# Two units' loads gated into each first projection, and the first two V casts written as a max over one element

## The chip, the cores and the metric

The kernel runs on one core of a Trainium2 chip. The metric is the device time of one execution in microseconds (us). Five engines run their own instruction streams: TensorE (PE, matmuls), VectorE (DVE), ScalarE (ACT), GpSimd (POOL) and SyncE (SP, which here only issues DMAs). They meet at semaphores. "PEld" is TensorE's weight load, which overlaps its matmuls.

## The reference

Cosine attention of 8 batches and 12 heads over 448 positions of 64, and then a feed-forward layer with the gate h·cos(h):

```python
q_n = q / (norm(q) + 1e-6);  k_n = k / (norm(k) + 1e-6)
attn = softmax(q_n @ k_n.T / 0.1)
x = (attn @ v)            # [8, 12, 448, 64] -> [3584, 768]
h = x @ w_in              # 768 -> 2048
out = (h * cos(h)) @ w_out   # 2048 -> 768
```

## The kernel before

**Units, pairs, batches.** The 12 heads of a batch are two *units* of six heads, 16 units in all (`u`); a unit is three *pairs* of heads, 48 pairs in all (`g`), six to a batch (`PB`). For a unit, `load(u, ...)` brings k and q into the f32 tile `raw[u % 2]` with two DMAs of 672 KB, and `load_v(u)` brings v into `vin[u % 2]` with one of 672 KB. All three are issued by SP. There are two buffers of each, so unit u + 2 can only be loaded when unit u's have been read.

**From raw to scores.** `norms` squares the pairs (`sq`, mostly on POOL, L686), sums the squares on DVE (`n`, L693), turns them into 1/norm with a Ln and an Exp on ACT (`lnn`, `rn`) and scales (`qks`, bf16, mostly on POOL, L712). From the tenth pair on (`BYPE`) a DMA transpose issued by SP makes `qkT` (L727); the first nine are transposed on PE and copied by DVE (L743). `scores` multiplies on PE (L752), ACT takes the exponent into `PX` (L757). `attend` multiplies with `va` (L774), which is v in bf16 with a column of ones; DVE divides by the sum (`rcp`, `xs`, L783 and L784), and a DMA transpose makes the pair's part of `xT` (L790), or PE and DVE do for every batch's last pair and the whole first batch (L798, L802).

**The V cast.** `copy_v(u)` converts `vin` to `va`. For the first two units that is a DVE `tensor_copy` (L662), for the others a POOL one.

**Projections.** `m1(b)`, the first projection, makes 96 matmuls for a batch (L815), in eight steps of twelve over three PSUM tiles (`SC0`, `SC1`, `AV`, the same tiles that scores and `attend` use); after each step ACT makes the cosine (`cosb`, L829) and DVE the product `gT` (L831). It runs at one place in the middle of the next batch's attention, after its second pair (`points`: pair 13 for batch 1, 19 for batch 2, and so on; batch 0's runs between the first batch and the second). `m2`, the second projection (L865), is put between the pieces of attention as filling work on PE, with its result copied by DVE to `osb` (L872) and stored by SP.

**What sets the order.** `Program` records every operation with its reads, writes and an assumed cost. `arrange` and `play` simulate the five engines and a shared DMA over these and fix, once, the order in which each engine runs its stream; among the operations that are ready, the one whose due time is earliest goes first. On the chip each engine then runs in that order, waiting at semaphores; nothing is reordered. Where the simulation sees PE idle for long, it puts matmuls of zeros there (`filler`, tile `zt`, L900), which compute nothing that is used: 92 of them. An edit of one operation therefore moves others all over the program.

**The loads' places.** The loads of the first two units come at the start. Those of units 2 and 3 follow the first batch, with the eight weight DMAs (POOL's queue, W1 and W2, f32 in memory and bf16 in SBUF). Unit 4 is loaded in pair 6. After that, units 5 to 15 are recorded one at a time, each in the second pair of the unit two before it, and go out as soon as their buffers are free.

Of the kernel before, what the change touches and what calls it, by code (L numbers as in the profile page):

```python
# [7 lines left out]
ALU = mybir.AluOpType  # L8
# [474 lines left out]
def bass_cosine_attention__then__act_gcu_kernel(  # L483
# [9 lines left out]
    B, NH, S, D = q.shape  # L493
# [121 lines left out]
    def dve(fn, reads, writes, cycles, lock=False, label="", bias=0.0):  # L615
        return P.op("DVE", fn, reads, writes, cost=0.15 + cycles / 960.0, lock=lock, label=label, bias=bias)
# [22 lines left out]
    def load(u, p0, p1, apart=False, eng="SP", behind=None):  # L639
        i = u % 2  # L640
        h = slice(2 * p0, 2 * p1)
        f = [lambda e, x=x, t=t: e.dma_start(
            rawv[i][:, h, NJ * x : NJ * x + NJ, :].rearrange("p h s d -> p h (s d)"), src(t, u, 2 * p0, 2 * (p1 - p0)))
            for x, t in enumerate((k, q))]
        for x in ((0,), (1,)) if apart else ((0, 1),):
            behind = P.ops[-1] if x == (1,) else behind
            behind = pooled[0] if eng == "POOL" else behind
            dma(eng, [f[y] for y in x], (), [("raw", i, p, y) for p in range(p0, p1) for y in x],
                "raw%d_%d_%s%s" % (i, p0, x, eng), 0.82 * (p1 - p0) * len(x), "load u%d p%d" % (u, p0), behind, 0.055)
            if eng == "POOL":  # L650
                pooled[0] = P.ops[-1]

    def load_v(u, eng="SP"):
        i = u % 2
        dma(eng, [lambda e: e.dma_start(vin[i].ap().rearrange("p (h c) -> p h c", h=UH), src(v, u, 0, UH))],
            (), [("vin", i)], "vin%d%s" % (i, eng), 2.4, "load v u%d" % u, pooled[0] if eng == "POOL" else None, 0.055)
        if eng == "POOL":
            pooled[0] = P.ops[-1]

    def copy_v(u):  # L660
        i = u % 2
        f = lambda e: e.tensor_copy(vav[i][:, :, 0:D], vinv[i])  # L662
        if u < 2:
            dve(f, [("vin", i)], [("va", i)], UH * NJ * D, label="va%d" % u)
        else:
            pool(f, [("vin", i)], [("va", i)], 1.46, label="va%d" % u)

# [136 lines left out]
    def m1(b, early=0, split=NKC, turn=TURN):  # L804
        table(SINSET)

        def names(gi):
            return [PHs[turn[gi]][0]]

        def step(gi, a, c0, c1):  # L810
            n, ph = 2 * gi + a, PHs[turn[gi]][1]

            def f(e):
                for c in range(c0, c1):
                    t = e.matmul(ph[:, a, 0:S], W1v[:, c, 128 * n : 128 * n + 128], xTv[b % 2][:, c, :],  # L815
                                 start=(c == 0), stop=(c == NKC - 1))
                return t

            P.op("PE", f, [("W1", n // 4)] + [("xT", b % 2, c) for c in range(c0, c1)], names(gi), cost=(c1 - c0) * MM,
                 mode="F", label="M1 %d.%d" % (b, n))  # L820

        for gi in range(early):
            for a in range(2):
                step(gi, a, 0, split)
        for gi in range(NF // 2):
            ph, cz = PHs[turn[gi]][1], gi % 2
            for a in range(2):
                step(gi, a, split if gi < early else 0, NKC)
            act(lambda e, ph=ph, cz=cz: e.activation(cosv[cz], ph[:, :, 0:S], ACT.Sin, bias=cst.ap()[:, 0:1], scale=1.0),  # L829
                names(gi) + ["cst0"], [("cos", cz)], 2 * S, "S", 1, label="sin%d.%d" % (b, gi))  # L830
            dve(lambda e, ph=ph, cz=cz, gi=gi: e.tensor_tensor(  # L831
                gTv[:, 2 * gi : 2 * gi + 2, S * (b % 2) : S * (b % 2) + S], ph[:, :, 0:S], cosv[cz], ALU.mult),
                names(gi) + [("cos", cz)], [("gT", b % 2, gi)], 2 * S, label="g%d.%d" % (b, gi))
        table(EXPSET)
# [48 lines left out]
    def after(o, *ops):  # L883
        for y in ops:
            o.deps.append((y, True))
# [49 lines left out]
    def pair(g):  # L935
        u, p = g // UP, g % UP
        if p == 0 and u >= 2 and u + 1 < NU:
            norms(u + 1, 0)
        grouped(both, g, 0)
        if g >= 1 and g != PB:  # L940
            attend(g - 1)
        if p == 0 and 2 <= u < NU - 1:
            copy_v(u + 1)
            if u == 2:
                load(4, 0, UP)
                load_v(4)
        if 3 <= u < NU - 2 and p == 1:
            load(u + 2, 0, UP)
            load_v(u + 2)
        if g + 2 < PB:  # L950
            norms((g + 2) // UP, (g + 2) % UP)
        if g + 1 < PB:
            grouped(transposes, g + 1)
        if BYPE <= g + 3 < NG:
            transposes(g + 3)
        grouped(both, g, 2)
# [34 lines left out]
    for g in range(PB, NG):  # L991
        pair(g)
        if g in points:
            m1(points[g])
            m2_add(points[g])
            m2_emit(None if points[g] < B - 2 else 8)
    attend(NG - 1)
# [42 lines left out]
```

## Time and profile before

| what | us |
|---|---|
| runs shown | 461.44, 462.76, 466.6 (median 462.76) |
| the profiled execution's own time | 465.73 |
| its span (first to last instruction) | 463.9 |
| PE busy, share of the span | 435.5, 94% |
| ACT, DVE, POOL busy | 263.5, 216.5, 195.0 |
| matmuls of zeros | 92, 23.6 us of PE's busy time |

The columns of the views that the prediction quotes are these. A *group* has line, engine, operation, output <- input, shapes, count, then busy us and mean ns of one, and the idle time of the engine just before them with what ended it. A *timeline* row has start (us from the span's start), length, engine, line, operation, tiles, count, and in brackets the idle time before it with what ended that. A *wait* row says who waited for whom: us in all, times, longest. A *window* row has the stretch A:B, its length, busy us (count) of the engines asked for, the clock that TensorE was granted (1.00 is full), the busy share of the DMA engines and GB/s. SPq is SP's stream of DMA issues; the time of such a row is that of issuing, not of the transfer. Buffer numbers are left out, so that `raw<-in_q_dram` is q of any unit.

The program falls into stages by what PE does: 0 to 45 us the first batch's attention, 45 to 66 the first projection of batch 0, then by turns the attention of a batch (about 28 us) and a first projection (about 20 us), which start at 104.2, 154.6, 207.4, 254.8, 303.4 and 352.7 us; from 396 us on the last projections.

### The profile page before, as it was taken

What the parts mean: (1) busy time and instruction counts of PE and PEld (TensorE: products, weight loads), DVE (VectorE), ACT (ScalarE), POOL (GpSimd) and SP (SyncE); (2) the same over time, 40 slices, a digit from 0 to 9 for tenths busy, and PEclk for the clock granted to TensorE, in tenths of its full rate; (3) what the DMA queues carried; (4) which work ended last, traced back from release to release, by engine and by line L of the source; (5) the groups of instructions that cost most, each with busy time, mean ns of one, the idle gap of its engine ahead of it and who ended that gap; (6) DMA issues with size and microseconds to landing.
All of it is one profiled execution on the core that took longest, in us unless ns stands there. A gap on an engine that the chain in (4) does not pass through costs nothing.

```text
span 463.9 us, 8849 instructions
## 1 busy us (share of the span) xinstructions
PE 435.5 (94%) x3800; PEld 235.8 (51%) x3800; DVE 216.5 (47%) x295; ACT 263.5 (57%) x319; POOL 195.0 (42%) x120
## 2 busy tenths in 40 slices
PE   8688999998899889999998999989999999999996
PEld 4355545554455435555554445545555555555663
DVE  4685672654732663356434562356431442244121
ACT  4467469874488537754678358743886168423000
POOL 1967448784475444673096309442560000000000
PEclk9799999999999999999999999989999999999999
DMA  8999994999349923992169806990481103101232
GB/s 221 236 236 220 248 253 96 279 187 245 98 65 256 210 65 72 232 239 90 37 144 227 223 0 132 224 236 4 86 137 52 36 8 92 45 0 35 79 92 69
DMA packets 95911, 63.87 MB, mean 138 GB/s; under 512 B 54912, under 2 KB 92288, under 8 KB 95872
## 3 DMA queue, kind: packets, MB, share of 16 engines
q1 hardware_dynamic: 90624, 57.02, 53.6%
q0 software_dynamic: 5248, 6.29, 7.8%
q8 instruction: 30, 0.49, 0.5%
q14 instruction: 9, 0.07, 0.1%
HBM read 45.61 MB, written 11.01 MB: 122 GB/s over the span
## 4 chain that ended last, share of the span: by engine, by line
PE 57%; DMA 14%; ACT 10%; DVE 7%; POOL 5%; issue 3%; SPq 3%; ACTq 0%
PE PO L865 20%; DMA raw<-in_q_dram 11%; PE SC L815 10%; PE AV L815 8%; PE AV L774 8%; PE SC L752 6%; ACT PX L757 6%; POOL qks L712 3%; DMA xT<-xs 3%; PE PO L900 2%; PE SC L865 2%; DVE gT L831 2%; DVE va L662 2%; SPq L727 2%; DVE n L693 2%
## 5 line engine op out<-in xcount | busy, mean ns | idle before, releaser
L757 ACT ACTIVATE PX<-SC 112x896 bf16<-112x896 f32 x192 | 164.8, 913 | 39.2 <-PE SC L752 39.0
L865 PE MATMUL PO<-W,gT 128*128 128x384 bf16 x816 | 148.8, 326 | 0.0
L712 POOL TENSOR_TENSOR qks<-raw,rn 112x1024 bf16<-112x1024 f32 x47 | 89.0, 1918 | 92.6 <-ACT rn L704 92.6
L815 PE MATMUL SC<-xT,W 128*128 128x448 bf16 x480 | 97.2, 357 | 8.8 <-DMA xT<-xs 6.9
L865 PEld LDWEIGHTS PO<-W,gT 128*128 128x128 bf16 x816 | 73.4, 98 | 57.4 <-issue 15.3
L686 POOL TENSOR_TENSOR sq<-raw 112x1024 bf16<-112x1024 f32 x42 | 78.5, 1892 | 41.1 <-DMA raw<-in_q_dram 41.1
L829 ACT ACTIVATE cosb<-SC,cst 128x896 f32<-128x896 f32 x40 | 40.2, 1006 | 68.1 <-PE SC L815 53.0
L815 PEld LDWEIGHTS SC<-xT,W 128*128 128x128 bf16 x480 | 46.4, 99 | 55.1 <-issue 14.4
L693 DVE TENSOR_REDUCE n<-sq 112x16 f32<-112x1024 bf16 (+1 forms) x49 | 58.3, 1192 | 33.6 <-POOL sq L686 27.2
L752 PE MATMUL SC<-qkT 64*128 64x448 bf16 x384 | 58.2, 358 | 7.1 <-DVE qkT L743 4.6
L815 PE MATMUL AV<-xT,W 128*128 128x448 bf16 x288 | 58.5, 352 | 5.2 <-DVE gT L831 4.8
L774 PE MATMUL AV<-va,PX 112*128 112x65 bf16 x1536 | 58.0, 194 | 1.6 <-DVE xT L802 1.2
L774 PEld LDWEIGHTS AV<-va,PX 112*128 112x128 bf16 x1536 | 52.5, 98 | 12.6 <-issue 10.8
L872 DVE COPY osb<-PO 128x384 f32<-128x384 f32 x51 | 28.2, 553 | 60.6 <-PE PO L865 60.5
L831 DVE TENSOR_TENSOR gT<-SC,cosb 128x896 bf16<-128x896 f32 x40 | 43.4, 1087 | 27.8 <-ACT cosb L829 24.1
L783 DVE RECIPROCAL rcp<-AV 112x8 f32<-112x8 f32 x48 | 9.9, 207 | 87.5 <-PE AV L774 87.5
L829 ACT ACTIVATE cosb<-AV,cst 128x896 f32<-128x896 f32 x24 | 24.2, 1007 | 40.0 <-PE AV L815 29.3
L815 PEld LDWEIGHTS AV<-xT,W 128*128 128x128 bf16 x288 | 27.4, 98 | 33.6 <-issue 7.1
L752 PEld LDWEIGHTS SC<-qkT 64*128 64x128 bf16 x384 | 15.0, 93 | 43.2 <-ACT PX L757 22.2
L784 DVE TENSOR_TENSOR xs<-AV,rcp 112x512 bf16<-112x512 f32 x48 | 33.2, 691 | 2.0
L831 DVE TENSOR_TENSOR gT<-AV,cosb 128x896 bf16<-128x896 f32 x24 | 26.1, 1086 | 17.1 <-ACT cosb L829 13.0
L662 POOL CAST va<-vin 112x1536 bf16<-112x1536 f32 x14 | 20.5, 1462 | 18.5 <-PE AV L774 17.9
(34 smaller groups left out, 143.4 us busy)
## 6 DMA issues: line engine op xcount, KB each, us to landing
vin<-in_v_dram SPq DMA_DIRECT2D x16, 672.0 KB, 8.2
raw<-in_k_dram SPq DMA_DIRECT2D x14, 672.0 KB, 5.9
raw<-in_q_dram SPq DMA_DIRECT2D x14, 672.0 KB, 8.4
W<-in_moe_w_in_dram POOLq DMA_DIRECT2D x4, 768.0 KB, 18.5
W<-in_moe_w_out_dram POOLq DMA_DIRECT2D x4, 768.0 KB, 18.9
out_dram<-osb SPq DMA_DIRECT2D x8, 336.0 KB, 3.1
out_dram<-osb SPq DMA_DIRECT2D x8, 288.0 KB, 2.7
out_dram<-osb SPq DMA_DIRECT2D x8, 240.0 KB, 3.0
```

Of the source, the lines that this page charges most:

```text
L662: f = lambda e: e.tensor_copy(vav[i][:, :, 0:D], vinv[i])
L686: pool(lambda e, x=x, y=y: e.tensor_tensor(y, x, x, ALU.mult), src_, dst, 0.1 + n * 1.78e-3, label="sq%d.%d" % (u, p))
L693: dve(lambda e, w=w: e.tensor_reduce(out=n2v[i][:, 2 * p : 2 * p + 2, w], in_=sqv[p][:, :, w, :], axis=mybir.AxisListType.X, op=ALU.add), ...
L712: f = lambda e, s0=s0, s1=s1: e.tensor_tensor(qksv[i][:, p, s0:s1, :, :].rearrange("p s h d -> p h s d"), rawv[i][:, h, s0:s1, :], bass.AP ...
L752: t = e.matmul(SCv[z][:, a, 0:S], qkT[k].ap()[r, NP * c : NP * c + 128], qkT[k].ap()[r, S : 2 * S], start=True, stop=True)
L757: act(lambda e: e.activation(PXv[j][:, c, 0 : 2 * S].rearrange("p (a s) -> p a s", a=2), SCv[z][0:NP, :, 0:S], ACT.Exp, scale=1.0 / TAU), ...
L774: t = e.matmul(AVv[:, a, n * x : n * x + n], PXv[j][:, c, k : k + 128], vav[i][:, NJ * (2 * p + a) + c, 0:n], start=(c == 0), stop=(c == N ...
L784: dve(lambda e: e.tensor_tensor(xsv[y].rearrange("p x h d -> p h x d"), AXv[:, :, :, 0:D], bass.AP(rcp[y], 0, [[NS, NP], [NJ, 2], [1, NJ], ...
L815: t = e.matmul(ph[:, a, 0:S], W1v[:, c, 128 * n : 128 * n + 128], xTv[b % 2][:, c, :], start=(c == 0), stop=(c == NKC - 1))
L829: act(lambda e, ph=ph, cz=cz: e.activation(cosv[cz], ph[:, :, 0:S], ACT.Sin, bias=cst.ap()[:, 0:1], scale=1.0), names(gi) + ["cst0"], [("c ...
L831: dve(lambda e, ph=ph, cz=cz, gi=gi: e.tensor_tensor(gTv[:, 2 * gi : 2 * gi + 2, S * (b % 2) : S * (b % 2) + S], ph[:, :, 0:S], cosv[cz], ...
L865: r = e.matmul(po[:, 0:HW], gTv[:, y, col : col + 128], W2v[:, y, HW * hf : HW * hf + HW], start=(y == 0), stop=(y == NF - 1))
```

## The change

Two edits.

1. The loads of units 6 to 15 are no longer issued one unit at a time as their buffers come free. They are recorded two units at a time behind `m1(points[g])`, units 6 and 7 in the first projection of batch 1, 8 and 9 in that of batch 2, up to 14 and 15 in that of batch 5, and each waits for the first step of that projection on PE (`after`). Units 0 to 5 stay as they were.
2. The first two V casts, DVE `tensor_copy` with f32 in and bf16 out, become `tensor_reduce` with max over an axis of one element: same input, same output, same values.

```diff
         if u < 2:
-            dve(f, [("vin", i)], [("va", i)], UH * NJ * D, label="va%d" % u)
+            dve(lambda e: e.tensor_reduce(
+                out=vav[i][:, :, 0:D], in_=vin[i].ap().rearrange("p (x d o) -> p x d o", d=D, o=1),
+                axis=mybir.AxisListType.X, op=ALU.max), [("vin", i)], [("va", i)], UH * NJ * D, label="va%d" % u)
         else:
...
-        if 3 <= u < NU - 2 and p == 1:
-            load(u + 2, 0, UP)
-            load_v(u + 2)
+        if u == 3 and p == 1:
+            load(5, 0, UP)
+            load_v(5)
...
         if g in points:
+            first = len(P.ops)
             m1(points[g])
+            first = [o for o in P.ops[first:] if o.eng == "PE"][0]
+            for u in (2 * points[g] + 4, 2 * points[g] + 5):
+                if u < NU:
+                    load(u, 0, UP)
+                    after(P.ops[-1], first)
+                    load_v(u)
+                    after(P.ops[-1], first)
             m2_add(points[g])
```

The assumed cost of the V cast is the same in both (`dve` with the same number of cycles). How the rows stand now, at three places; line numbers in the changed program are two higher from L664 on.

DVE in the first batch, around the first V cast (`qkT1` is the second pair's transposed q and k, `xs0` the first pair's result). Before:

```order
L743 COPY qkT0<-PO2 128x896
L662 CAST va0<-vin0 112x24x64
L743 COPY qkT1<-PO2 128x896
L783 RECIPROCAL rcp0<-AV 112x8
L693 TENSOR_REDUCE n21<-sq0 112x16
```

and with the change:

```order
L745 COPY qkT0<-PO2 128x896
L664 TENSOR_REDUCE va0<-vin0 112x24x64
L745 COPY qkT1<-PO2 128x896
L785 RECIPROCAL rcp0<-AV 112x8
L695 TENSOR_REDUCE n21<-sq0 112x16
```

Nothing moves here; the cast has another form. The second cast moves by one place: it stood ahead of the third copy to `xT0` and now stands behind it.

SP around the first projection of batch 2 (`xT0<-xs3` and `xT0<-xs4` are the parts of `xT` that this projection needs last, `raw0` and `raw1` units 8 and 9). Before:

```order
L790 DMA_TRANSPOSE xT0<-xs3 128x4x112
L642 DMA raw0<-in_k_dram 112x6x256
L642 DMA raw0<-in_q_dram 112x6x256
L727 DMA_TRANSPOSE qkT3<-qks1 128x8x112
L727 DMA_TRANSPOSE qkT4<-qks1 128x8x112
L790 DMA_TRANSPOSE xT0<-xs4 128x4x112
L727 DMA_TRANSPOSE qkT5<-qks1 128x8x112
L642 DMA raw1<-in_k_dram 112x6x256
L642 DMA raw1<-in_q_dram 112x6x256
L655 DMA vin1<-in_v_dram 112x6x256
```

and with the change, where the loads wait for the projection's first step:

```order
L792 DMA_TRANSPOSE xT0<-xs3 128x4x112
L729 DMA_TRANSPOSE qkT3<-qks1 128x8x112
L792 DMA_TRANSPOSE xT0<-xs4 128x4x112
L729 DMA_TRANSPOSE qkT4<-qks1 128x8x112
L729 DMA_TRANSPOSE qkT5<-qks1 128x8x112
L878 DMA out_0_dram<-osb0 48x768
L878 DMA out_0_dram<-osb0 80x768
L792 DMA_TRANSPOSE xT1<-xs0 128x4x112
L642 DMA raw0<-in_k_dram 112x6x256
L642 DMA raw0<-in_q_dram 112x6x256
L655 DMA vin0<-in_v_dram 112x6x256
L642 DMA raw1<-in_k_dram 112x6x256
```

Unit 8's load stood three transposes ahead of `xT0<-xs4` and unit 9's close behind it; both now stand behind all transposes of this attention.

DVE in the same projection (`n20` and `n21` are the sums of squares of the even and the odd unit, the eight `gT` the steps of the projection). Before:

```order
L693 TENSOR_REDUCE n20<-sq1 112x16
L693 TENSOR_REDUCE n20<-sq2 112x16
L831 TENSOR_TENSOR gT<-SC0,cosb0 128x2x448
L831 TENSOR_TENSOR gT<-SC1,cosb1 128x2x448
L693 TENSOR_REDUCE n21<-sq0 112x16
L831 TENSOR_TENSOR gT<-AV,cosb0 128x2x448
L693 TENSOR_REDUCE n21<-sq1 112x16
L831 TENSOR_TENSOR gT<-SC0,cosb1 128x2x448
L693 TENSOR_REDUCE n21<-sq2 112x16
L831 TENSOR_TENSOR gT<-SC1,cosb0 128x2x448
```

and with the change:

```order
L833 TENSOR_TENSOR gT<-SC0,cosb0 128x2x448
L833 TENSOR_TENSOR gT<-SC1,cosb1 128x2x448
L833 TENSOR_TENSOR gT<-AV,cosb0 128x2x448
L833 TENSOR_TENSOR gT<-SC0,cosb1 128x2x448
L833 TENSOR_TENSOR gT<-SC1,cosb0 128x2x448
L695 TENSOR_REDUCE n20<-sq0 112x16
L833 TENSOR_TENSOR gT<-AV,cosb1 128x2x448
L695 TENSOR_REDUCE n20<-sq1 112x16
L833 TENSOR_TENSOR gT<-SC0,cosb0 128x2x448
L695 TENSOR_REDUCE n20<-sq2 112x16
```

The even unit's sums move from ahead of the projection to behind its fifth step, and the odd unit's three move out of the projection, to the first three pairs after it. On POOL the odd unit's third squaring now stands behind two scalings of the even unit and a V cast; on ACT the odd unit's Ln (`lnn1`) now stands in the third pair after the projection, between its second and third exponent, where it stood in the first. PE's program has 78 matmuls of zeros instead of 92: 11 instead of 20 behind the first projection of batch 0, three fewer ahead of the very first transpose.

## The prediction, on record before the run

> **What bounds the kernel now.** I read the page first, then who waited for whom, then busy time by stages, then the timelines of the stages in which PE stands still.
>
> The page's row on PE:
>
> ```profile
> PE 435.5 (94%) x3800; PEld 235.8 (51%) x3800; DVE 216.5 (47%) x295; ACT 263.5 (57%) x319; POOL 195.0 (42%) x120
> ```
>
> PE bounds the kernel: of 463.9 us it is idle for 28.4. So the question is where it is idle, or busy with zeros, and whether the change fills that. From the list of waits, four rows (us in total, times, longest):
>
> ```profile
> PE SC L815 <- DMA xT<-xs: 6.9, 4, 2.2
> ...
> PE AV L815 <- DVE gT L831: 4.8, 5, 1.6
> PE SC L752 <- DVE qkT L743: 4.6, 3, 4.0
> ...
> PE SC L815 <- DVE gT L831: 1.5, 1, 1.5
> ```
>
> Three kinds of wait hold most of the idle time. A first projection waits for its input `xT` (6.9), its steps wait for DVE's `gT` to give back a PSUM tile (4.8 + 1.5), and at the start the scores wait for a DVE copy (4.6). Each has a place.
>
> The start, timelines of DVE, POOL, ACT and PE in that order:
>
> ```profile
> 13.25 6.46 DVE L662 CAST va<-vin 112x1536 bf16<-112x1536 f32 x1
> 19.64 0.61 DVE L743 COPY qkT<-PO 128x896 bf16<-128x896 bf16 x1
> ...
> 28.97 2.66 DVE L662 CAST va<-vin 112x1536 bf16<-112x1536 f32 x1
> ...
> 32.38 1.20 DVE L693 TENSOR_REDUCE n<-sq 112x16 f32<-112x1024 bf16 x1
> ```
>
> ```profile
> 16.66 1.90 POOL L686 TENSOR_TENSOR sq<-raw 112x1024 bf16<-112x1024 f32 x1
> 18.50 2.45 POOL L889 DMA_DIRECT2D W<-in_moe_w_in_dram  x2
> ...
> 30.77 2.62 POOL L712 TENSOR_TENSOR qks<-raw,rn 112x1024 bf16<-112x1024 f32 x1
> ```
>
> ```profile
> 13.96 3.34 ACT L757 ACTIVATE PX<-SC 112x896 bf16<-112x896 f32 x4 [1.25 <-PE SC L752]
> ...
> 20.99 1.90 ACT L757 ACTIVATE PX<-SC 112x896 bf16<-112x896 f32 x2 [3.69 <-PE SC L752]
> ```
>
> ```profile
> 21.86 1.94 PE L774 MATMUL AV<-va,PX 112*128 112x65 bf16 x32
> ...
> 26.89 1.19 PE L774 MATMUL AV<-va,PX 112*128 112x65 bf16 x32
> ```
>
> The first V cast takes 6.46 us and ends at 19.71, 1.15 us after POOL's squaring ends at 18.56: it stood waiting for POOL. The copy that the second pair's scores need is behind it, and ACT has no exponent to do for 3.69 us. A sum (TENSOR_REDUCE), on the other hand, ran at 32.38 for 1.20 us in the middle of a POOL instruction (30.77 to 33.39), not longer than its mean below: that form does not wait.
>
> The projections, from PE's timeline: those of batches 2 and 5, and that of batch 6, ahead of which no load is left.
>
> ```profile
> 154.58 4.70 PE L815 MATMUL SC<-xT,W 128*128 128x448 bf16 x24 [1.77 <-DMA xT<-xs]
> ...
> 303.39 6.38 PE L815 MATMUL SC<-xT,W 128*128 128x448 bf16 x24 [2.20 <-DMA xT<-xs]
> ...
> 352.67 4.70 PE L815 MATMUL SC<-xT,W 128*128 128x448 bf16 x24 [0.16 <-ACT PX L757]
> ```
>
> All four `xT` waits stand ahead of batches with a load of 2 MB in flight in the pairs before; without loads 0.16 us is left. And inside batch 2's projection, from the chain of waits and from DVE's timeline:
>
> ```profile
> 154.11 9.25 DMA raw<-in_q_dram
> ```
>
> ```profile
> 165.35 1.22 DVE L693 TENSOR_REDUCE n<-sq 112x16 f32<-112x1024 bf16 x1 [3.90 <-POOL sq L686]
> 166.49 1.08 DVE L831 TENSOR_TENSOR gT<-AV,cosb 128x896 bf16<-128x896 f32 x1
> ```
>
> Unit 9's q lands 9.25 us after its issue, POOL squares, and DVE, which runs in order, stands at the sum for 3.90 us with a finished projection step behind it. That is the gT wait.
>
> **Part 1, the V casts.** The price of the new form, from the groups by shape:
>
> ```profile
> L693 DVE TENSOR_REDUCE n<-sq 112x16 f32<-112x1024 bf16 x47 | 56.9, 1213 | 30.7 <-POOL sq L686 27.2 <-ACT sq L682 3.4
> ...
> L693 DVE TENSOR_REDUCE n<-sq 112x8 f32<-112x512 bf16 x2 | 1.4, 686 | 2.9 <-ACT sq L682 2.8
> ```
>
> 512 elements more cost 527 ns, 1.03 ns each; 1536 elements give 1213 + 527 = 1.74 us. These rows make one output of 64 inputs; the new form makes 1536 outputs of one. If an output cost as much as an input it would be 1.74 + 1.58 = 3.3 us; below 1.74 nothing speaks for it. I take 1.74, since eight outputs more are not seen in the step between the two rows. The cast then runs from 13.25 to 15.0, and the copy of the second pair's `qkT` ends at 15.6. What is late next is ACT: its four exponents of the first pair end at 17.30, so the next begin there instead of at 20.99, 3.7 us earlier. Behind the stall PE ran at half clock:
>
> ```profile
> 22.00:24.00 2.00, 2.00 (x37) 0.50 1.17 247
> 305.00:307.00 2.00, 2.00 (x7) 0.50 1.10 313
> ```
>
> (window rows; the clock is the figure after the count). The first AV block took 1.94 us instead of the 1.19 of the next: 0.75 more. I take 3.7 + 0.75 = **4.5 us**. Bounds: 5.9, if all of the second cast (2.66 - 1.74 = 0.9) and the three matmuls of zeros that go from the very start (0.5) count too; 0, if the front is held by its transfers (first rival).
>
> The Trainium skill, "VectorE: DVE Perf Modes", section "The perf-mode tier table", speaks against this edit: a tensor_reduce has no fast mode, where an f32 copy in SBUF runs two elements a cycle. By that alone each cast would lose some 0.8 us, an estimate from that page's factor of two on 1.74, and the sum would be 1.6 worse; in this trace the first cast took 6.46, so the slower form is the shorter one. Its page "SBUF — State Buffer", section "Who interferes with whom", gives a reason that agrees with the 6.46 and the 1.20: such a copy and GpSimd lock each other out of a shared port for a whole instruction, and a tensor_reduce on trn2 never takes it.
>
> **Part 2, matmuls of zeros.** The same rows by stage, of L900 alone:
>
> ```profile
> 66.30:104.20 37.90, 4.38 (x20) 1.71 (x20) 1.00 0.82 192
> ```
>
> 20 of them, 4.38 us, stand behind batch 0's projection, in a stage in which PE has work of the second projection to do; with the change 11 are left, 9 x 0.219 = **2.0 us** less. Bounds 0 (PE then waits at that place, for weights) and 2.0.
>
> **Part 3, the moved loads.** What goes: the four `xT` waits, 6.9 less 4 x 0.16 = **6.3**, since behind the change each attention looks as that before 352.67; bounds 3.5 (half) and 6.9. The gT waits, 6.3 less the one of batch 0's projection, which keeps its loads:
>
> ```profile
> 63.96 2.43 PE L815 MATMUL AV<-xT,W 128*128 128x448 bf16 x12 [0.74 <-DVE gT L831]
> ```
>
> so 6.3 - 0.7 = **5.6**, bounds 2.8 (half) and 5.6: no sum stands ahead of the fifth `gT` any more. And at 303.39 the 24 matmuls took 6.38 instead of 4.70, at the half clock of the second window row above, behind the longest of the `xT` waits: **1.7**, bounds 0 and 1.7. "TensorE: Matmul & The Clock Gate", section "What's actually happening" of the Trainium skill, ties half clock to an idle window of about 3.4 us; by that the 2.20 us wait was no cause, the 1.7 would stay, and the gain would be 16.9 instead of 18.6. Here the clock fell behind 2.20 and not behind 1.77, so I keep it.
>
> What comes: loads wait on PE at SP. Queued behind them on SP are only stores and the transposes of pairs after the projection, so nobody waits for that. The new place is late for the units, though. When does the odd unit land? The rate in batch 1's projection:
>
> ```profile
> 112.00:120.00 8.00, 7.27 (x39) 1.00 1.09 278
> ```
>
> The gate opens after twelve matmuls, 12 x 0.19 (24 in the 4.70 above) = 2.3 us into the projection. The size of one transfer, from the page's DMA issues:
>
> ```profile
> raw<-in_k_dram SPq DMA_DIRECT2D x14, 672.0 KB, 5.9
> ```
>
> Up to the odd unit's q there are five, 3.44 MB, at 278 GB/s 12.4 us, and some 2 us of latency (my allowance): 16.7. POOL squares twice, 3.8: 20.5 us after the projection's start. Then POOL's new order:
>
> ```profile
> 130.58 3.76 POOL L712 TENSOR_TENSOR qks<-raw,rn 112x1024 bf16<-112x1024 f32 x2 [8.04 <-ACT rn L704]
> 134.28 1.46 POOL L662 CAST va<-vin 112x1536 bf16<-112x1536 f32 x1
> ```
>
> and PE's third pair behind that projection, which ended at 125.7:
>
> ```profile
> 136.27 0.66 PE L752 MATMUL SC<-qkT 64*128 64x448 bf16 x4
> ```
>
> The scalings start 4.9 us after the projection's end, at 23.1 with its 18.2 us (96 x 0.19), so the squares are there 2.6 us early. Two scalings, the V cast, the third square (1.90) and the sum (1.21) end 13.2 after the projection's end; ACT's Ln for it stands behind two exponents of the third pair, whose scores start 10.6 after; with 0.4 for the first two of these matmuls and 1.90 for two exponents (the row at 20.99) ACT comes there at 12.9. It waits 0.3 us, five times: **1.5** lost; bounds 0, if PE has filling work meanwhile, and 5 x 1 = 5.
>
> Sum: 4.5 + 2.0 + 6.3 + 5.6 + 1.7 - 1.5 = **18.6 us**. The profiled execution took 465.73 us, so its like would take 447.1, with a span of 445.3. It lies 3.0 above the median of the runs shown, 462.76, by which I predict: 462.76 - 18.6 = 444.2.
>
> **Rivals.**
>
> *The front is held by transfers.* For: by the page's 40 slices of 11.6 us (busy tenths) the DMA engines have next to no pause in the first six, and unit 3's load, which batch 0's projection sums, is slow; the second row is from the chain of waits:
>
> ```profile
> DMA  8999994999349923992169806990481103101232
> ```
>
> ```profile
> 39.16 19.20 DMA raw<-in_q_dram
> ```
>
> Against: it is issued when POOL has scaled the first batch, which moves forward with the rest. If it lands at 58.4 all the same, DVE's sums hold batch 0's projection and the 4.5 are gone: gain 14.1, 448.7.
>
> *The `xT` waits stay*, because other transposes and not the loads hold SP's queue: gain 18.6 - 6.3 - 1.7 = 10.6, 452.2. Against it stands 352.67.
>
> *The odd unit is late, slower than before.* Loads pile up in one place; beyond 2.6 us of lateness each us moves ACT's Ln and the exponents behind it in five batches. Decisive point: to lose the 18.6 and 4.6 more (1%) takes 23.2 / 5 = 4.6 on top, 7.2 in all, so 3.44 MB in 19.6 us, 175 GB/s instead of 278. Then 467.4 or more. No saturated stretch quoted here is that slow; batch 1's attention shows 192 with a DMA share of 0.82.
>
> *It does not do what it says.* The order is a plan; if PE's other neighbours (ACT, POOL) close the gaps that open, the gain is the front's at most and lost again: 462.
>
> **How the numbers follow.** Forecast 0.57, front held 0.15, `xT` waits stay 0.12, no change 0.09, odd unit late 0.07. A difference of 1% is about what these runs can tell from none. Faster by over 1%, below 458.1: the first three, 0.84. Same 0.09, slower 0.07. All upper ends give 5.9 + 2.0 + 6.9 + 5.6 + 1.7 = 22.1, 440.7, and 1.3 less for the spread of the runs below their median: 439. The upper end must hold the second and third cases with half a gT wait lost (452.2 + 2.8): 455. Outside lie the last two cases.
>
> **What would show it.** The first cast: one row near 1.7 us, and ACT's second exponents near 17.3. The wait row of PE for `xT`: under 1 us. That for gT: about 0.7. Stages of first projections near 18.4 us. PE's granted clock 1.00 in all of them. A wait of ACT's `lnn` for DVE's `n` in the third pair behind each projection, near 0.3 us. It is wrong if the wait for raw's transfers moves onto ACT, or if PE waits for scores behind the projections.

## The result and the profile after

On the same chip the kernel before took 463.83 us (median; 461.44 to 466.6) and the changed kernel 446.51 us (445.1 to 447.41). The ratio is 0.962, 95% interval 0.956 to 0.969: 17.3 us less. The prediction was 444.2, with 439 to 455 as its range. The profiled execution took 445.67 us, 20.06 less than that of before (465.73), and its span is 443.9 instead of 463.9. The steps are compared on these two spans, 20.0 us apart.

The page's row on PE, of after:

```profile
PE 428.4 (97%) x3786; PEld 232.1 (52%) x3786; DVE 211.0 (48%) x295; ACT 264.2 (60%) x319; POOL 193.7 (44%) x120
```

PE is idle for 15.5 us instead of 28.4, and busy for 7.1 less. The list of waits of after:

```profile
PE SC L754 <- ACT PX L759: 3.5, 7, 1.8
...
PE SC L817 <- ACT PX L759: 1.1, 7, 0.2
...
PE SC L817 <- DVE gT L833: 0.4, 1, 0.4
```

The `xT` waits (6.9) are gone. Of the gT waits (4.8 + 1.5) there is 0.4 left, in batch 0's projection, whose loads were not moved. One row is larger than before: PE waits for ACT's exponents, once for 1.8 us.

The front, DVE's timeline and then PE's, of after:

```profile
12.18 1.74 DVE L664 TENSOR_REDUCE va<-vin 112x1536 bf16<-112x1536 f32 x1
13.84 0.62 DVE L745 COPY qkT<-PO 128x896 bf16<-128x896 bf16 x1
...
24.14 1.74 DVE L664 TENSOR_REDUCE va<-vin 112x1536 bf16<-112x1536 f32 x1
```

```profile
58.31 2.43 PE L817 MATMUL AV<-xT,W 128*128 128x448 bf16 x12
...
145.16 4.70 PE L817 MATMUL SC<-xT,W 128*128 128x448 bf16 x24 [0.16 <-ACT PX L759]
...
283.50 4.70 PE L817 MATMUL SC<-xT,W 128*128 128x448 bf16 x24 [0.16 <-ACT PX L759]
```

Each cast is one row of 1.74 us. The last twelve matmuls of batch 0's projection stand at 58.31; before they stood at 63.96. The later projections, here those of batches 2 and 5, begin behind a wait of 0.16 us.

The windows of PE by stage (the columns after the stretch are its length, PE's busy time with its count, granted clock, DMA share, GB/s): batch 1's attention, then everything from its projection to the start of batch 6's, then the rest. Before:

```profile
66.39:104.24 37.85, 37.03 (x408) 1.00 0.82 193
104.24:352.67 248.43, 234.89 (x2138) 0.99 0.66 143
352.67:463.90 111.23, 106.62 (x752) 1.00 0.18 49
```

After:

```profile
60.74:99.05 38.31, 35.36 (x399) 1.00 1.08 202
99.05:331.87 232.82, 231.46 (x2132) 1.00 0.68 156
331.87:443.90 112.03, 107.27 (x756) 1.00 0.18 48
```

Up to the end of batch 0's projection 5.65 us are gained (66.39 to 60.74); in batch 1's attention 0.5 are lost; in the long middle 15.6 are gained; in the tail 0.8 are lost. In the middle PE's idle time goes from 13.54 to 1.36 us, so 12.2 of the 15.6 are idle time and 3.4 are shorter busy time.

### The profile page after: what moved, and what is told of

Its sections match the earlier page's. It is cut to its first block, busy times and chain, and to the rows that moved or that the text cites. A ratio compares the mean times of both kernels' runs of the same rounds, so it can differ in the third digit from the quotient of the medians.

```text
span 443.9 us, 8809 instructions
## 1 busy us (share of the span) xinstructions
PE 428.4 (97%) x3786; PEld 232.1 (52%) x3786; DVE 211.0 (48%) x295; ACT 264.2 (60%) x319; POOL 193.7 (44%) x120
## 4 chain that ended last, share of the span: by engine, by line
PE 82%; ACT 6%; POOL 4%; DMA 3%; DVE 2%; issue 1%; SPq 1%; ACTq 0%; POOLq 0%
PE PO L867 27%; PE SC L817 21%; PE AV L817 12%; PE AV L776 10%; PE SC L754 9%; ACT PX L759 4%; DMA raw<-in_q_dram 3%; POOL qks L714 3%; PE SC L867 2%; POOL sq L688 1%; SPq L642 1%; PE AV L800 1%; PE AV L867 1%; ACT L608 1%; DVE n L695 1%
## 5 line engine op out<-in xcount | busy, mean ns | idle before, releaser
L817 PE MATMUL SC<-xT,W 128*128 128x448 bf16 x480 | 95.7, 352 | 1.9 <-ACT PX L759 1.1
L754 PE MATMUL SC<-qkT 64*128 64x448 bf16 x384 | 57.0, 356 | 4.8 <-ACT PX L759 3.5
L831 ACT ACTIVATE cosb<-AV,cst 128x896 f32<-128x896 f32 x24 | 24.2, 1007 | 39.2 <-PE AV L817 27.4
## 6 DMA issues: line engine op xcount, KB each, us to landing
W<-in_moe_w_in_dram POOLq DMA_DIRECT2D x4, 768.0 KB, 17.6
```

Of the source, the lines that this page charges most:

```text
L754: t = e.matmul(SCv[z][:, a, 0:S], qkT[k].ap()[r, NP * c : NP * c + 128], qkT[k].ap()[r, S : 2 * S], start=True, stop=True)
```

## The experiments

Two of the kernels have, row for row, the order of another on every engine, because the assumed cost of both forms of the cast is the same: the casts alone stand in the order of before, the loads alone in that of the changed kernel. Two further ones keep such an order for other reasons, without the wait and without the zeros. In the rest the planner arranges the other rows anew, so their times hold such shifts too.

**The casts alone.** The kernel before, with

```diff
-            dve(f, [("vin", i)], [("va", i)], UH * NJ * D, label="va%d" % u)
+            dve(lambda e: e.tensor_reduce(
...
+                axis=mybir.AxisListType.X, op=ALU.max), [("vin", i)], [("va", i)], UH * NJ * D, label="va%d" % u)
```

> The V casts as a max over one element alone; all loads stay where they were before, and every engine's order is that of the kernel before. Theory (the front's gain goes through): the first cast is one row of 1.74 us instead of 6.46, batch 0's projection ends near 60.7 us of the span instead of 66.3, and the stages behind it are those of before, so the run is 5.0 to 5.7 us faster than before, near 458.5. My prediction's own term was 4.5. Rival (the front is held by transfers further on): the loads of units 4 and 5 do not come forward with it, batch 1's projection starts at 104.2 as before, and the run is within 1 us of before. The waits for xT and gT stay in both, near 6.9 and 6.3 us in all.

Measured: 460.47 us beside 465.39 of the kernel before, ratio 0.987 (0.981 to 0.994). The cast took 1.74 us and batch 0's projection ended at 60.64, so the front gained its 5.75 us, but batch 1's attention grew by 1.0 and the gain is 4.9 in the medians and 4.2 in the profiled spans (459.7). The waits stayed, with 4.8 us for `xT` and 6.5 for gT. The theory holds for the front; the time falls a little short of it, and what takes that comes up below.

**The loads alone.** The changed kernel, with the first edit only:

```diff
-            dve(lambda e: e.tensor_reduce(
...
-                axis=mybir.AxisListType.X, op=ALU.max), [("vin", i)], [("va", i)], UH * NJ * D, label="va%d" % u)
+            dve(f, [("vin", i)], [("va", i)], UH * NJ * D, label="va%d" % u)
```

> The moved and gated loads alone; the two casts are copies as before, and every engine's order is that of the changed kernel. Theory (the parts add): the first cast takes about 6.5 us again, batch 0's projection ends near 66.3, everything behind it is as in the changed kernel and 5.65 us later: 12 us faster than before in the medians (17.3 less 5.65), so near 452; in profiled spans 443.9 + 5.65 = 449.6. No wait of PE for xT over 0.3 us, gT waits below 1 us. Rival (the parts share a gain, or need each other): over 2 us away from that, because ACT's wait for unit 5's load in batch 1's attention (1.8 us on PE in the changed kernel) comes or goes with the front.

Measured: 449.16 us, ratio 0.964 (0.959 to 0.970), a gain of 16.2. Taken alone, then, the parts gain 4.9 and 16.2, and together 17.3: they do not add, and the rival is nearer. In medians the gap of 3.8 is no more than three comparisons of 2.5 to 3 us to both sides leave open; in the profiled spans it is 1.8 (4.2 and 17.6 against 20.0). The profile says where. First, the copy got through sooner here. DVE's timeline, and POOL's, of the loads alone:

```profile
12.45 1.31 DVE L662 CAST va<-vin 112x1536 bf16<-112x1536 f32 x1
...
24.74 4.08 DVE L662 CAST va<-vin 112x1536 bf16<-112x1536 f32 x1
```

```profile
24.24 1.90 POOL L686 TENSOR_TENSOR sq<-raw 112x1024 bf16<-112x1024 f32 x1
26.10 1.90 POOL L712 TENSOR_TENSOR qks<-raw,rn 112x1024 bf16<-112x1024 f32 x1
```

The first cast, whose neighbours on DVE and POOL stand as in the kernel before, took 1.31 us and not 6.46, and the second 4.08 and not 2.66. The second ends at 28.82, 0.82 after POOL's two computations end at 28.00: so long does the copy itself take, and the rest is standing behind POOL. Two more casts bear this out: the first one here ended 0.80 behind a scaling on POOL, the second one of the kernel before 0.82 behind a squaring. The 6.46 us fit less well: that cast ended 1.15 behind POOL, and why it did not get through at its start, while POOL issued two DMAs (12.94 to 14.79), no run shows. Second, the front's lead here was small (batch 0's projection ended at 65.03): behind the cast of 4.08 us PE stood 2.34 for the next scores, and the AV block at 34.30 took 1.94 us instead of 1.19. Batch 1's attention took 36.15 us instead of 38.31.

**Which of the two loads.** Only the even units gated into the projections, the odd ones as before:

```diff
-        if u == 3 and p == 1:
-            load(5, 0, UP)
-            load_v(5)
+        if p == 1 and (u == 3 or 3 < u < NU - 2 and u % 2 == 1):
+            load(u + 2, 0, UP)
+            load_v(u + 2)
...
-            for u in (2 * points[g] + 4, 2 * points[g] + 5):
+            for u in (2 * points[g] + 4,):
```

> The changed kernel, but only the even units 6 to 14 are gated into the projections; the odd units 7 to 15 are loaded as before, in the second pair of the unit two before. It tells which of the two moved loads pays for which wait. Theory (the even unit's load, which stood ahead of the last transposes into xT, made the xT waits, and the odd unit's, whose sums stood ahead of a gT, the gT waits): xT waits gone (below 1 us), gT waits back (3 to 6 us), so 449.5 to 452.5. Rival (any load beside the transposes makes the xT waits): xT waits of 3 us or more although only the odd unit's load is left there, and over 453.

and its mirror, with `u % 2 == 0` above and `2 * points[g] + 5` below:

> The mirror of the last one: only the odd units 7 to 15 are gated into the projections, the even units 6 to 14 are loaded as before. Theory: the xT waits come back (4 to 7 us, with the half clock behind the longest up to 1.7 more), the gT waits stay away (below 1 us): 451 to 455. Rival (any load beside the transposes, or the odd one's alone, made the xT waits): xT waits below 1 us, and a time within 1.5 us of the changed kernel's 446.5.

Measured: the even units alone 445.71 us (ratio 0.956, 0.951 to 0.962), the odd units alone 459.47 (0.987, 0.981 to 0.993). The list of waits, of the even ones and then of the odd ones:

```profile
PE SC L817 <- ACT PX L759: 1.1, 7, 0.2
...
PE AV L817 <- DVE gT L833: 0.5, 1, 0.5
```

```profile
PE SC L817 <- DMA xT<-xs: 4.9, 2, 2.7
PE AV L817 <- DVE gT L833: 2.5, 2, 2.2
PE SC L817 <- DVE gT L833: 2.0, 2, 1.6
```

My attribution fell. With the even units' loads moved, both kinds of wait are gone, though the odd units' loads were not gated at all; with only the odd ones moved both stay. The odd unit's gate pays nothing: in batches 2, 4 and 5 of the kernel before, that load already stood behind the last part of `xT` in SP's order, and in batch 3 it moves there when the even unit's is held.

**Without the wait.** The loads recorded two units at a time at the projections, as in the change, but not held:

```diff
                     load(u, 0, UP)
-                    after(P.ops[-1], first)
                     load_v(u)
-                    after(P.ops[-1], first)
```

> The changed kernel, with the loads recorded two units at a time at the projections as there, but without the wait on PE. In SP's order the even unit's load then stands again ahead of the last transpose into xT (raw0 between xT0<-xs3 and xT0<-xs4), and the odd unit's directly behind the transposes, as in the kernel before. Theory (the gate, and of it the even unit's, is what the gain comes from): xT waits 4 to 7 us and gT waits 3 to 6 us are back, 457 to 461, no better than the casts alone. Rival (the place of recording does it, two units at a time): xT waits below 1 us, time within 2 us of 446.5.

Measured: 461.97 us, ratio 0.989 (0.982 to 0.996). The plan that comes out is that of the casts alone, row for row on every engine: the planner orders by due times, and where a load is recorded changes nothing. Without the wait the whole edit of the loads is nothing. The theory holds, though time and waits (7.6 us for `xT`, 7.3 for gT) lie a little past its ranges. One plan's waits differ that much from profile to profile.

**The odd units, later.** Only the odd units gated, at the seventh step of eight:

```diff
-            first = [o for o in P.ops[first:] if o.eng == "PE"][0]
+            first = [o for o in P.ops[first:] if o.eng == "PE"][12]
```

> The kernel with only the odd units gated, with their gate at the seventh of the projection's eight steps instead of the first. In DVE's order all three sums of the odd unit (n21) then stand behind the eighth gT; those of the even unit stay among the first three. Theory (the gT waits come from sums of the odd unit that are ordered inside the projection and wait for its load, wherever that load is issued): gT waits fall from 4.5 us to below 1.5, the xT waits stay at 4 to 7 us, since the even unit's load still stands ahead of the last transpose; 1 to 4 us faster than the kernel with the odd units gated at the first step (459.5), so 455 to 458.5. Rival (the gT waits come with the even unit's load, late itself, and its sums): gT waits stay at 3 us or more, time within 1 us of 459.5.

Measured: 450.66 us, ratio 0.969 (0.964 to 0.974). Neither expected the time: the `xT` waits, which both left in place, are gone. In the plan the even unit's load, not gated, now stands behind the fifth and last part of `xT` that goes through SP, presumably because with the odd unit's work later the planner issued that part earlier. So this kernel gives the cause of the `xT` waits more sharply than the gate did. Over all profiles, for batches 2 to 5:

| the even unit's load in SP's order | kernels | places | `xT` waits |
|---|---|---|---|
| ahead of the last part or parts of `xT` | before, casts, no gate, odd | 16 | 13, of 1.1 to 2.7 us |
| behind the last part | changed (twice), loads, even (twice), even late, late, unit 5 on POOL, no zeros, odd late | 40 | none |

The names are more than the orders: before, casts and no gate have one order on SP, and so have changed, loads and no zeros. It is two orders against six.

SP's timeline shows how: before, ahead of batch 2's projection,

```profile
140.97 1.67 SPq L790 DMA_TRANSPOSE xT<-xs  x1
142.69 0.58 SPq L642 DMA_DIRECT2D raw<-in_k_dram  x1
143.31 0.52 SPq L642 DMA_DIRECT2D raw<-in_q_dram  x1
143.87 5.81 SPq L727 DMA_TRANSPOSE qkT<-qks  x2
149.74 2.35 SPq L790 DMA_TRANSPOSE xT<-xs  x1
```

and DVE's row for the input of that last part, of before:

```profile
142.59 0.69 DVE L784 TENSOR_TENSOR xs<-AV,rcp 112x512 bf16<-112x512 f32 x1
```

The same places after the change, SP and then DVE:

```profile
136.16 1.26 SPq L792 DMA_TRANSPOSE xT<-xs  x1
137.47 3.42 SPq L729 DMA_TRANSPOSE qkT<-qks  x2
```

```profile
134.78 0.69 DVE L786 TENSOR_TENSOR xs<-AV,rcp 112x512 bf16<-112x512 f32 x1
```

Before, the part's input was ready at 143.28 and its transpose was issued at 149.74, 6.5 us later, behind the load and two transposes that took 5.81 us to issue. After, it was ready at 135.47 and issued at 136.16. It also landed later behind the load; the views of these two DMAs, before and then after:

```profile
DMA to landing us min/median/max: 4.6/4.6/4.6
```

```profile
DMA to landing us min/median/max: 2.4/2.4/2.4
```

From readiness to landing the part took 11.1 us, and now 3.1. In the changed kernel the projection starts 9.7 us after the part is ready (135.47 to 145.16). By these figures the delay at SP with the short landing, 8.9, would still have fitted: here it takes both.

The new order also puts the part ahead of one of the two transposes of `qkT`, so these might be the cause by themselves. Two places speak against it. With unit 5's squaring on POOL (a run that comes below), batch 5's last part stands behind two such transposes and no load:

```profile
273.27 3.06 SPq L729 DMA_TRANSPOSE qkT<-qks  x2
276.38 1.26 SPq L792 DMA_TRANSPOSE xT<-xs  x1
```

The two took 3.06 us to issue, the part landed 2.4 us after its issue, and PE did not wait for it. With only the odd units gated, one transpose stands between the load and the last part in batch 4: it took 2.96 us, the part landed 7.2 us after its issue at 238.88, and PE waited 2.73.

Of the 3.2 us of gT waits in the kernel with the odd units gated later, 2.79 come from one place. DVE's timeline and PE's, in batch 1's projection:

```profile
107.09 1.22 DVE L695 TENSOR_REDUCE n<-sq 112x16 f32<-112x1024 bf16 x1 [7.76 <-POOL sq L688]
108.23 1.08 DVE L833 TENSOR_TENSOR gT<-SC,cosb 128x896 bf16<-128x896 f32 x1
```

```profile
109.46 6.01 PE L817 MATMUL SC<-xT,W 128*128 128x448 bf16 x24 [2.79 <-DVE gT L833]
```

Here it is the even unit's first sum that stands ahead of the first `gT`; of the odd unit no sum stands in the projection, and in batches 2 to 5 no projection waits for `gT`. So the theory holds for four batches and the rival for one: what makes a gT wait is a sum of either unit that is ordered among the `gT` ahead of its load's landing. A sum there does no harm when its data are there. DVE's timeline in batch 2's projection, of after:

```profile
157.81 1.09 DVE L833 TENSOR_TENSOR gT<-SC,cosb 128x896 bf16<-128x896 f32 x1 [1.18 <-ACT cosb L831]
158.82 1.21 DVE L695 TENSOR_REDUCE n<-sq 112x16 f32<-112x1024 bf16 x1
160.08 1.09 DVE L833 TENSOR_TENSOR gT<-AV,cosb 128x896 bf16<-128x896 f32 x1
```

With the change the even unit's sums stand behind the fifth, sixth and seventh `gT` there and fit into pauses of DVE that were there anyway; the odd unit's follow behind the last `gT`. With the even units' gate alone, too, the odd unit's sums come behind those of the even one, and so are out of the way without a gate of their own.

**The new wait.** Unit 5's third squaring on POOL instead of ACT:

```diff
-                square(u, x, "A" if u in (3, 4, 5) and x == 2 else "P")
+                square(u, x, "A" if u in (3, 4) and x == 2 else "P")
```

> The changed kernel, with the third squaring of unit 5 on POOL instead of ACT. It tells what the wait in batch 1's attention cost (ACT stood 2.65 us at this squaring for unit 5's load, and PE 1.8 us for the exponent behind it). Theory (this wait swallowed what the front gained): that attention, 60.7 to 99.05 in the changed kernel, becomes 1.5 to 2.5 us shorter, ACT has no wait for raw there, and the run is 444.0 to 445.0. Rival (unit 5's load itself is late, and whoever squares it makes the next stage wait): the attention stays within 0.5 us of 38.4 and the time within 0.5 of 446.5.

What it is about, from ACT's timeline of after:

```profile
84.19 1.06 ACT L684 ACTIVATE sq<-raw 112x1024 bf16<-112x1024 f32 x1 [2.65 <-DMA raw<-in_q_dram]
85.15 3.32 ACT L759 ACTIVATE PX<-SC 112x896 bf16<-112x896 f32 x4
```

and from PE's:

```profile
86.19 0.37 PE L754 MATMUL SC<-qkT 64*128 64x448 bf16 x2 [1.81 <-ACT PX L759]
```

ACT runs in order and stands 2.65 us at a squaring for unit 5's load, with the exponents behind it. Measured: batch 1's attention, 60.75 to 97.46, is 1.6 us shorter, and ACT has no such wait there; yet the time is 445.7 and not 444.0 to 445.0, ratio 0.957 (0.951 to 0.963), span 443.8. Half of the theory holds: that wait cost what was said. The 1.6 us are lost again in this plan: of the later stages, projection to projection, three are 0.7, 1.6 and 0.4 us longer than in the changed kernel, and PE waits once for 1.4 us for a transposed `qkT`. The casts alone have the same squaring waiting 1.70 us; the loads alone, whose front is later, 0.47.

**Later loads.** The gate six half steps later, for all ten units:

```diff
-            first = [o for o in P.ops[first:] if o.eng == "PE"][0]
+            first = [o for o in P.ops[first:] if o.eng == "PE"][6]
```

> The changed kernel, with the gate of all ten units' loads six half steps later in the projection: they are issued 6.9 us later, near 9.4 us after its start instead of 2.5. It prices the rival in the prediction by which the odd unit is late. By that rival only 2.6 us of slack lie ahead of POOL's scalings, and the changed kernel has used them up (the odd unit's squares end right ahead of the scalings in its batches 1 and 2), so each us shows on PE: up to 5 x 6.9 = 34 us slower than the changed kernel, at least 5 x 4.3 = 21, so 467 to 481. Theory now (the units loaded here are wanted by PE only in the next batch's attention, some 20 us later, and the planner moves the scalings along): POOL's squares and scalings come 5 to 7 us later, PE waits for nothing new, 446 to 449.

Measured: 446.13 us, ratio 0.957 (0.951 to 0.963). POOL's timeline in batch 2, whose projection starts at 143.24 here, and that of after, where it starts at 145.16:

```profile
168.75 1.89 POOL L688 TENSOR_TENSOR sq<-raw 112x1024 bf16<-112x1024 f32 x1 [3.84 <-DMA raw<-in_q_dram]
170.59 1.90 POOL L714 TENSOR_TENSOR qks<-raw,rn 112x1024 bf16<-112x1024 f32 x1
```

```profile
164.56 3.74 POOL L688 TENSOR_TENSOR sq<-raw 112x1024 bf16<-112x1024 f32 x2 [3.49 <-DMA raw<-in_q_dram]
168.46 3.76 POOL L714 TENSOR_TENSOR qks<-raw,rn 112x1024 bf16<-112x1024 f32 x2 [0.16 <-ACT rn L706]
```

The loads went out 8.1 us after the projection's start instead of 2.5, the odd unit's first squaring came at 25.5 instead of 19.4, the scalings at 27.4 instead of 23.3. PE lost nothing. The rival's 21 us and more did not come. The planner knew of the lateness and put the odd unit's second squaring behind the scalings, so what an unplanned lateness costs is not shown; but the scalings came 4.1 us later and PE did not wait, and that refutes the slack of 2.6 us in the prediction.

**Without the zeros.** The changed kernel less the 11 matmuls of zeros behind batch 0's projection, all else in the same order:

```diff
-            for a, b in self.gaps:
+            end0 = max(o.end for o in self.ops if o.label.startswith("M1 0."))
+            for a, b in [x for x in self.gaps if x[1] <= end0]:
```

> The changed kernel without the 11 matmuls of zeros behind batch 0's projection (at 63.1 and 65.2 us); every other row of every engine is in the same order. My prediction counted fewer of these as a gain, 0.219 us each. Theory of the prediction (they stand on the path): 11 x 0.219 = 2.4 us faster than the changed kernel, 444.1. Rival (they fill time in which PE would wait for ACT's exponents anyway): the zeros' time turns into waits of PE for PX, and the time stays within 0.7 us of 446.5; if the clock falls behind those waits, up to 1 us slower.

Measured: 445.56 us, ratio 0.956 (0.950 to 0.962). PE's timeline behind batch 0's projection:

```profile
64.44 0.36 PE L755 MATMUL SC<-qkT 64*128 64x448 bf16 x2 [0.85 <-ACT PX L760]
65.24 0.36 PE L755 MATMUL SC<-qkT 64*128 64x448 bf16 x2 [0.44 <-ACT PX L760]
66.55 0.36 PE L755 MATMUL SC<-qkT 64*128 64x448 bf16 x2 [0.94 <-ACT PX L760]
67.35 0.36 PE L755 MATMUL SC<-qkT 64*128 64x448 bf16 x2 [0.44 <-ACT PX L760]
67.65 1.65 PE L777 MATMUL AV<-va,PX 112*128 112x65 bf16 x32
```

Where zeros stood PE now waits for ACT: the four waits are 2.67 us, of which 0.62 were there with the zeros too (0.41 and 0.21). The AV block behind them starts 6.6 us after the projection's end (67.65 less 61.05), exactly as with the zeros (67.34 less 60.74). The zeros filled waits; the rival holds, and so does its last clause: behind the four waits the clock fell. The granted clock was 0.60 from 67.6 to 70.0 us, and the AV block and the two groups behind it took 1.65, 0.93 and 2.15 us where they took 1.19, 0.56 and 1.47 with the zeros, 1.5 us more. In this profile the stage was still 0.9 shorter in all, since ACT's squaring for unit 5, at 83.61, waited 0.36 us here and 2.65 there. The times decide nothing: this run's median lies 0.9 below the changed kernel's and its ratio 0.006, less than these comparisons can tell, and as far as they go the theory's 2.4 us are not excluded.

**The best of these, side by side.** The changed kernel and the even units alone once more, and the even units with the later gate (`[6]` as above):

> The changed kernel once more, beside the next run on the same chip. 445 to 447.

> The kernel with only the even units gated once more, beside the changed kernel on the same chip. Theory (the odd unit's gate pays nothing, and the period from one projection to the next is 45.6 us instead of 46.1): 1.0 to 1.5 us faster than the changed kernel, about 0.3%. Rival: the same within 0.5 us.

> Only the even units gated, six half steps later in the projection. Theory (neither the odd unit's gate nor the moment of the even unit's load inside the projection holds PE): 444.5 to 446.5, as with the gate at the first step. Rival (the loads' landing inside the projection matters): 2 us or more off.

Measured on one chip: 446.96, 446.52 and 446.85 us, ratios 0.962, 0.961 and 0.962, each about 0.005 wide to both sides. The second run takes back the 1 us by which the even units alone had seemed ahead, and the later gate, 0.35 us past its theory's range, is far from its rival's 2 us. No version beats the changed kernel by anything that these runs can tell. The second profile of the changed kernel has no `xT` wait either, but one gT wait of 0.93 us, in batch 1's projection.

## Why the prediction was right, and where it was not

| term | forecast | in the profiles |
|---|---|---|
| front, the casts | 4.5 | 5.65 |
| zeros in batch 1's attention | 2.0 | 0; the stage is 0.5 longer |
| `xT` and gT waits | 6.3 + 5.6 | 12.2 of idle time in the middle |
| half clock behind the `xT` wait, other busy time | 1.7 | 3.4 |
| ACT's Ln behind the projections | -1.5 | 0 |
| tail | 0 | -0.8 |
| sum | 18.6 | 20.0 |

*The casts.* The price, 1.74 us from two rows of sums, was exact. The front gained 1.15 us more than the sum and stays below its upper bound of 5.9, which counted the second cast and the zeros at the very start. The page of the Trainium skill that spoke against the edit ("VectorE: DVE Perf Modes", section "The perf-mode tier table") is borne out in its own terms: the copy that got through needed 0.82 us, about half of the 1.74. What decides is the waiting, as the lock in the Trainium skill's page "SBUF — State Buffer", section "Who interferes with whom", has it: the second cast of the loads alone ended 0.82 us behind POOL's last computation. The gain was not a matter of 6.46 against 1.74, though: with the copy in both, and nearly the same order around it, the pair of casts took 9.1 us in one profile and 5.4 in another.

*The zeros.* This step failed: "9 x 0.219 = 2.0 us less", on the ground that PE had other work. PE's busy time in that stage did fall, by 1.67 us, but its idle time rose by 2.13. The zeros stood in waits for ACT's exponents, as the run without the 11 that are left shows (the nine that went were not tried by themselves); and the stage got a new wait of 1.81 us, which I had placed as a danger ("wrong if the wait for raw's transfers moves onto ACT") but not priced. It comes from the front's own gain: unit 5's load did not move forward as far as ACT's squaring of it, and ACT stood 2.65 us there. This is one of two reasons why the two edits, measured alone, sum to more than both together. By the profiles batch 1's attention makes 1.1 us of the gap (1.0 lost with the casts alone, 1.7 gained with the loads alone, 0.5 lost with both), and the front 1.5 (5.75 and 1.36 alone, 5.65 with both); 0.8 go the other way behind them.

*The loads.* The two large terms came as forecast, 11.9 against 12.2. The mechanism of the gT waits, a sum ordered among the `gT` and waiting for its load, is shown by the rows at 107.09 and 109.46 above, and that in batch 2 no sum stands ahead of the fifth `gT` any more by that at 158.82. For the `xT` waits the prediction named the load in flight. That is one half: in batch 2 the last part landed 4.6 us after its issue instead of 2.4. The other is the load's place in SP's order ahead of that part, which was issued 6.5 us after it was ready. What the prediction did not see is that one of the two loads is enough: the even units' gate alone gives the whole gain.

*The half clock.* PEclk is 1.00 in the middle, and the first projections' matmuls at SC and AV are 2.0 us shorter there (94.57 to 92.56, of which one matmul in the window's count is 0.2). The rest is about 0.8 of the scores (35.56 to 34.79 in the same windows), which I had not counted, and four matmuls of the second projection, 0.8, that moved into the tail, which is 0.8 longer.

*ACT's Ln.* The 1.5 did not come. The wait of ACT that it stands for did, in four batches, with 0.46 to 0.75 us (130.81 is the first), but PE did not wait for it. The odd unit's squares came at 16.4 to 19.7 us after the projections' start, which leaves the forecast landing of 16.7 up to 3 us short, but they are wanted by PE only in the next batch's attention. The 2.6 us were the distance to a row in POOL's order and no slack of PE's, so the slower rival built on it had no basis; the later loads show that.

*The other rivals.* The front was not held by unit 3's transfers: POOL's squaring of that unit moved from 58.43 to 52.77 us with the rest. That the `xT` waits stay because of other transposes is refuted: they are gone, and two transposes without a load made none.

## What to carry to other kernels

In a queue that issues in order, look at what stands between an urgent small transfer and the moment it is ready: there a load of no urgency cost 1 to 3 us per batch, by slower issues behind it and a slower landing, and moving that one load gained as much as the whole edit of the loads. A due-time planner ignores where a load is recorded, so only a real dependence moves it. Before counting the removal of filler as gain, find out what its engine would wait for without it; and price a slack from the row that finally needs the data, not from the next row in some engine's plan.

## What the hardware showed unasked

*Half clock needs no long wait, and the wait's length alone does not decide.* Behind waits of PE of 1.98 and 2.07 us (casts alone), 2.20 (before), 2.36 (no gate) and 2.73 (odd units) the next 24 matmuls took 6.4 us; behind 1.95 and 2.25 (no gate) and 2.15 (odd units) they took 4.70. Several short waits do it too: without the zeros four of 0.44 to 0.94 us, 2.67 in all within 3.8 us, brought the clock down behind them. Two rows of the run without the gate:

```profile
205.19 6.35 PE L817 MATMUL SC<-xT,W 128*128 128x448 bf16 x24 [2.36 <-DMA xT<-xs]
...
254.69 4.70 PE L817 MATMUL SC<-xT,W 128*128 128x448 bf16 x24 [2.25 <-DMA xT<-xs]
```

The Trainium skill, "TensorE: Matmul & The Clock Gate", section "What's actually happening", has a free-running window of about 3.4 us. That it runs free would fit the overlap between 1.98 and 2.25; that a whole idle window is needed doesn't fit, since none of these waits was longer than 2.8 us. What else counts was not tried.

*Loads land later in a crowd, and it can cost nothing.* The page's DMA issues, before and then after:

```profile
raw<-in_q_dram SPq DMA_DIRECT2D x14, 672.0 KB, 8.4
```

```profile
raw<-in_q_dram SPq DMA_DIRECT2D x14, 672.0 KB, 12.0
```

With six transfers behind one gate the median landing went from 8.4 to 12.0 us, in the faster kernel.
